# A transformer block on one core: when the transfers are issued, and from which queue

## The chip, the cores and the metric

The kernel runs on one core of one Trainium2 chip. The metric is the time of one execution in device microseconds (us). A core has a matrix engine (PE, with its weight loads as PEld), a vector engine (DVE), a scalar engine (ACT), a general engine (POOL) and a sync engine (SP) that only issues transfers. Each engine takes its instructions strictly in the order of its program. Transfers can be issued by SP and by ACT; in the profile these issues stand under SPq and ACTq.

## The reference

One pre-norm block: attention with 32 heads of 20 columns over a causal window of 256 rows, then a gated feed-forward part. S = 2048 rows, D = 640, F = 1536, all in f32.

```python
def _A_ref(x, wqkv, wo):
    H = 32; Dh = D // H; W = 256
    q, k, v = ...                                   # x @ wqkv, split by heads
    scores = jnp.einsum("bhqd,bhkd->bhqk", q, k) * (Dh ** -0.5)
    mask = (idx[:, None] - idx[None, :] >= 0) & (idx[:, None] - idx[None, :] < W)
    p = _softmax(jnp.where(mask[None, None], scores, -1e9), axis=-1)
    o = jnp.einsum("bhqk,bhkd->bhqd", p, v)
    return o.transpose(0, 2, 1, 3).reshape(B, S, D) @ wo
def _B_ref(x, w_gate, w_up, w_down):
    return (_gelu(x @ w_gate) * (x @ w_up)) @ w_down
h = x + _A_ref(_layernorm(x), wqkv, wo)
out = h + _B_ref(_layernorm(h), w_gate, w_up, w_down)
```

## The kernel before

The rows are cut into 16 blocks of 128 (numbered 0 to 15) and 8 chunks of two blocks. Every f32 operand of a large product is split into two f16 parts, high and low, and a product is made as three f16 products; the weights are split on the chip (`w0h`, `w0l` for q, `w1` for k, `w2` for v, `w3` for the output projection), each scaled by a power of two (`sw`) that is found from its largest element (`am`).

For a chunk the kernel normalizes the rows (`lstx`, `lmvx`, `lyx` are the steps of it, `x_lane` is its code), transposes them on PE (`tp` and, for blocks 1 and 3, `rb`) and splits them into `xh` (a cast on ACT) and `xl` (a difference on DVE). It multiplies by the q and k weights into `mm`, reads the result out as `qks` (high part by ACT, low part by DVE), and writes it to DRAM (`qk00` is chunk 0's q, `qk01` its k, `qk10` chunk 1's q, and so on) by transfers that ACT issues. Six transfers on SP read the q back into `qT`, six the k into `kT`, in the layout that the heads need (`stack`, L654). Two rows of `kT` come from the constant tile `big`, written once. Then a first pass over the scores finds the row maxima (`ra`, `rb` <- `kT`, `qT`; `junk` and `mxs` on DVE), the maxima are added into `qT` as two more rows (`qT<-mT`, issued by ACT), and a second pass makes the scores, the exponentials (`pt`, ACT, with a mask on POOL), and the product with v (`pv`). At the end of a block stand the output projection, the residual (`ht`, loaded again from x, L908) and a store of the sum to `h_dram` (L934). The feed-forward part works from `h_dram`: its first piece beside the last blocks, the rest after about 625 us.

All instructions are recorded through one helper, so the profile gives them all one line, L184; they are told apart by the names of their tiles. The order of each engine is fixed when the program is built. A planner (`Clock`, `Engine.cost`, `Lane.start`) keeps an estimated time for each engine, notes for every region of a tile when it was last written and read (`box`, `note`, `latest`), and issues from a list of generators the first one whose condition (`need`) is met at the estimated time. A generator that only issues transfers yields `("sync",)` and such a condition. So a change of an estimate or of a condition moves instructions on all engines; the estimates are no times of the chip.

One more thing sets the order of transfers. SP and ACT together have eight completion counters, DMAHW0 to DMAHW7, that are given to their transfers in turn, in the order of the plan. A transfer that takes a counter for the second time first waits, on its own engine, until the transfer that had it last has landed. A transfer of SP can so wait for one of ACT, and the other way round; the planner does not count this wait.

At the start SP loads, in this order, x blocks 0 and 1 (`xt`, `pt`), the five slices of the q weights (into `qT`, used as room), five of the k weights (`gu`), x block 2, five of the v weights (`v`), x block 3, then the two transfers `kT<-big`, and when its slots are free slices of the output weights (`wsl`). Block 4's load (`xt`) is a step of the generator `x_lane` for the later blocks.

Of the kernel before, what the change touches and what calls it, by code (L numbers as in the profile page):

```python
# [18 lines left out]
DRAM = bass.MemoryType.DRAM  # L19

S, D, H, DH, F = 2048, 640, 32, 20, 1536
P = 128
# [8 lines left out]
CB = 4  # L31
# [19 lines left out]
class Clock:  # L51
# [16 lines left out]
    @staticmethod  # L68
    def box(ap):

        t = ap.tensor
        size = mybir.dt.size(ap.dtype)
        (ps, pn), *free = [tuple(x) for x in ap.ap]
        if ps:
            p0, f0 = divmod(ap.offset, ps)
        else:
            p0, f0 = 0, ap.offset
        n = 1 + sum((c - 1) * abs(st) for st, c in free)
        step, count = max(((abs(st), c) for st, c in free if c > 1), default=(n, 1))
        run = n - (count - 1) * step  # L80
        if run >= step:
            run, count = n, 1
        return t.name, (p0, p0 + pn, f0 * size, (f0 + n) * size, run * size, step * size, count)
# [91 lines left out]
class Engine:  # L175
# [20 lines left out]
    def cost(self, op, out, ins):  # L196
        n = out.free_size()
        if op == "dma_start":
            size = n * out.partition_size() * mybir.dt.size(out.dtype)
            return size / (300e3 if mybir.dt.size(out.dtype) == 4 else 150e3)  # L200
        half = mybir.dt.size(out.dtype) == 2 and ins and mybir.dt.size(ins[0].dtype) == 2
        if self.name == "tensor":
            n = ins[1].free_size()
            if op == "transpose":
                n = ins[0].partition_size()
            passes = 1 if mybir.dt.size(ins[0].dtype) == 2 else 2 if op == "transpose" else 4
            rows, cols = ins[0].partition_size(), out.partition_size()
            mode = "full" if op == "transpose" else "row" if rows <= 64 else "col"
            mode = "full" if mode == "col" and cols > 32 else mode
            k = self.clock  # L210
            switch, k.mode = SWITCH * (k.mode != mode), mode
            at = (ins[0] if mode == "row" else out).start_partition()
            beside, k.half = mode != "full" and at > k.half and not switch, at
            if beside:
                return 0.004
            return switch + k.warmth(max(n * passes / 2400, 0.027), rows) + 0.0027
        if self.name == "vector":
            m = max([n] + [i.free_size() for i in ins])
            if op == "tensor_copy" and half or op == "tensor_scalar" and m > 320:
                return (0.065 if half else 0.185) + 0.00053 * m  # L220
            return 0.065 + 0.00106 * m + 0.06 * (op == "scalar_tensor_tensor" and len(ins) == 3)
        if self.name == "scalar":
            return 0.00084 * n + (0.05 if op == "copy" or len(ins) == 1 else
                                  0.14 if ins[0].space == PSUM else 0.18)
        if self.name == "gpsimd":
            if op == "memset":
                return 0.06 + 0.0008 * n
            return 0.46 if n == 1 else 0.06 + (0.00105 if op == "affine_select" else 0.00203) * n
        raise NotImplementedError(self.name)
# [3 lines left out]
def block_kernel(ctx: ExitStack, tc: tile.TileContext, x, wqkv, wo, wg, wu, wd, out):  # L233
    nc = Clock(tc.nc)
# [5 lines left out]
    stage = ctx.enter_context(tc.tile_pool(name="stage", bufs=1))  # L240
# [5 lines left out]
    opened, pos = Counter(), Counter()  # L246
# [13 lines left out]
    INF = float("inf")  # L260
# [5 lines left out]
    NR = 4  # L266
    NW, AHEADQ = 3, 6
    SPREAD = 0
    SLICES = 3
# [7 lines left out]
    def need(*reads, slots=(), when=None, eng="tensor"):  # L277

        def f():
            if when and not when() or any(opened[n] >= banks[n] for n in slots):  # L280
                return INF
            return max([nc.ready(reads, eng)]
                       + [nc.slot(psum, n, banks[n]) for n in slots])
        return f
# [4 lines left out]
    def on(eng, *reads, when=None, after=None):  # L289
        f = need(*reads, when=when, eng=eng)  # L290
        if after is not None:
            return (eng,), lambda: max(f(), nc.others(after, eng))
        return (eng,), f
# [18 lines left out]
    class Weight:  # L312
# [21 lines left out]
        def load_slices(self, turn):  # L334
            self.sliced = True
            for i in range(self.shape[0]):
                yield ("sync",), need(when=lambda: pos["taken"] < pos["used"] + SLICES, eng="sync")
                t = nc.tile(stage, [P, D], F32, "wsl", SLICES)[:, :self.shape[1]]
                nc.sync.dma_start(t, self.src[:, i, :])
                self.raw[turn, i] = t  # L340
                pos["taken"] += 1
            self.loaded = True
# [64 lines left out]
    W = {}  # L407
# [125 lines left out]
    RV, RK = 5, 6  # L533
# [50 lines left out]
    def x_lane(blocks, lane):  # L584

        for j in blocks:
            c = C[j // 2]
            if j > 1:
                yield on("vector", when=lambda: W["k"].scaled)
            if j >= NR and j == blocks[0]:  # L590
                yield ("sync",), need(eng="sync", when=lambda: W["v"].scaled)
                load_x(j)
            if j >= NR and j + 1 < NB:
                yield ("sync",), lambda: max(0.0, nc.slot(att, "xt", 2))
                load_x(j + 1)

            def dst():
                if c.x is None:
                    c.x = tuple(nc.tile(wq, [P, KC, CW], F16, n, 3) for n in ("xh", "xl"))
                return tuple(t[:, :, B[j].cols] for t in c.x)  # L600

            yield from layernorm(B[j].x, lane, None, None, dst,
                                 lambda: j < 6 or c.x or C[j // 2 - 3].used == 4,
                                 lambda: B[j].x, tp="rb" if j in (1, 3) else "tp")
            B[j].ready = True

    def load_x(j):
        if 0 < j < NR:
            t = at("pt", [P, 4, 3, P], F32, 3).rearrange("p a b c -> p (a b c)")
            B[j].x = t[:, 0:D]  # L610
        else:
            B[j].x = at("xt", [P, D], F32)
        nc.sync.dma_start(B[j].x, x[j * P:(j + 1) * P, :])
# [38 lines left out]
            side.append((LATE, stack(c, which, d)))  # L652

    def stack(c, which, d):  # L654
        yield ("sync",), need(when=lambda: c < 2 or B[2 * c - 3].scored, eng="sync")
        if which == 0:
            C[c].qT = at("qT", [P, H // 2, CW], F16)
            for b in (2 * c, 2 * c + 1):
                B[b].mx = at("mxs", [P, H], F32, 4)
            to = C[c].qT  # L660
        else:
            s = 2 * c % RK
            to = kT[:, :, s:s + 2, :].rearrange("p i r n -> p i (r n)")
        for par in range(2):
            for m, i in enumerate(((0, 0, 1), (0, 1, 0))[which]):
                rows = slice(64 * par + DH * m, 64 * par + DH * m + DH)
                nc.sync.dma_start(to[rows], d[i].rearrange("(a d i) n -> a d i n", a=2,
                                                           d=DH)[par])
        C[c].stacked += 1
        if C[c].stacked == 2:  # L670
            for b in (2 * c, 2 * c + 1):
                for pr in range(H // 2):
                    heapq.heappush(maxq, (b, pr))
# [89 lines left out]
    row = []  # L763
# [142 lines left out]
        woq.append(j)  # L906

    def residual(j):  # L908
        yield ("sync",), need(when=lambda: j < 2 or B[j - 2].wrote
                              and (j >= CB + 2 or B[j - 2].normed), eng="sync")  # L910
        B[j].h = at("ht", [P, D], F32)
        nc.sync.dma_start(B[j].h, x[j * P:(j + 1) * P, :])

# [11 lines left out]
    def wo_out(j, nh, ps):  # L925
        b = B[j]
        cs = slice(nh * 320, nh * 320 + 320)
        yield on("vector", ps)
        nc.vector.scalar_tensor_tensor(b.h[:, cs], ps, hsc, b.h[:, cs], op0=ALU.mult, op1=ALU.add)
        done("mm")  # L930
        b.halves += 1
        if b.halves < 2:
            return
        nc.sync.dma_start(h_dram[j * P:(j + 1) * P, :], b.h)  # L934
        pos["h"] += 1
        b.wrote = True
# [250 lines left out]
    class Lane:  # L1187
# [11 lines left out]
        def start(self, now):  # L1199
# [11 lines left out]
            if ffpools[1]:  # L1211
                back = FFBACK.get(name, OUT)
            return (all(nc.t[e] <= now + back for e in self.engs if e != "sync")
                    and self.need() <= now + 0.1)

    load_x(0)
    load_x(1)
    qraw = [at("qT", [P, H // 2, CW], F16).bitcast(F32).rearrange("p a n -> p (a n)")
# [2 lines left out]
    for i, n in enumerate("qkv"):  # L1221
        W[n].load(rooms[n])
        if i:
            load_x(i + 1)
    for par in range(2):
        nc.sync.dma_start(kT[64 * par + 60:64 * par + 62].rearrange("p i r n -> p (i r) n"),
                          big[0:2, None, :].to_broadcast([2, RK * H // 2, P]))
    lanes = [x_lane([0], "x"), x_lane([1], "xb"), x_lane([2], "xc"), x_lane([3], "xd"),
             x_lane(range(NR, NB), "x"),
             *(scale_lane([i], str(i)) for i in range(NW)), split_lane(),  # L1230
# [91 lines left out]
```

## Time and profile before

| | |
|---|---|
| three executions, us | 1089.8, 1084.14, 1089.83 (median 1089.8) |
| the profiled execution | 1087.55 us, span of the profile 1085.8 us, mean granted PE clock 0.984 |
| PE busy | 1032.3 us, 95% of the span |
| DVE, ACT, POOL busy | 670.0, 457.1, 173.0 us |
| the chain that ended last | PE 75%, DVE 12%, DMA 6%, ACT 4% of the span |
| transfers | 77.01 MB, 71 GB/s over the span |

The profile is that of one execution. A row of its timeline gives the start, the duration, the engine, the line, the operation and the tiles (out <- in), and in brackets how long the engine had been idle and what it had waited for. A row of SPq or ACTq is an engine that issues transfers (a following `x6` means six of them in a group, and the duration is from the first issue to the end of the last). The clock is the share of full speed that PE was granted.

### The profile page before, as it was taken

How to read it: one execution, taken by the hardware profiler on the slowest of the kernel's cores; microseconds unless marked ns; L12 is line 12 of the kernel's file. 1: busy time of each engine (PE TensorE's matmuls, PEld its weight loads, DVE VectorE, ACT ScalarE, POOL GpSimd, SP SyncE). 2: the span in 40 equal slices, each digit the busy share in tenths (PEclk: the TensorE clock that was granted, in tenths of full speed). 3: DMA queues.
4: the chain of work that ended last, by engine and by line, in shares of the span. 5: the costliest groups of instructions: out<-in, count | busy, mean ns of one | idle time of the engine just before them, and what ended most of it. 6: DMA issues, size and time to landing. Idle time of an engine off the chain costs nothing.

```text
span 1085.8 us, 25031 instructions
## 1 busy us (share of the span) xinstructions
PE 1032.3 (95%) x10122; PEld 631.6 (58%) x10122; DVE 670.0 (62%) x1993; ACT 457.1 (42%) x904; POOL 173.0 (16%) x286
## 2 busy tenths in 40 slices
PE   5368999999999999999999999999999999999998
PEld 3335567666676666676655564555555555545546
DVE  8567899978887687777779389723622263222323
ACT  3213566666666666665767644310211121110110
POOL 1000112332332333333333300000000000000000
PEclk9779999999999999999999999999999999999999
DMA  6526535424233221414052034002000020001001
GB/s 242 137 54 177 130 117 155 128 62 100 64 91 84 73 66 51 88 56 110 34 172 75 14 109 145 1 1 97 1 1 1 25 73 1 1 1 50 1 1 49
DMA packets 63639, 77.01 MB, mean 71 GB/s; under 512 B 6500, under 2 KB 42596, under 8 KB 62564
## 3 DMA queue, kind: packets, MB, share of 16 engines
q1 hardware_dynamic: 40420, 64.67, 20.4%
q10 hardware_dynamic: 23104, 10.75, 3.6%
q8 instruction: 79, 1.29, 0.5%
q14 instruction: 36, 0.29, 0.1%
HBM read 54.07 MB, written 20.97 MB: 69 GB/s over the span
## 4 chain that ended last, share of the span: by engine, by line
PE 75%; DVE 12%; DMA 6%; ACT 4%; issue 2%; SPq 1%; ACTq 0%; POOL 0%; DVEq 0%; POOLq 0%
PE mm L184 57%; PE pv L184 6%; DVE junk L184 4%; PE rb L184 4%; PE tp L184 4%; PE ra L184 4%; ACT pt L184 2%; DMA qk<-qks 2%; DMA kT<-qk 2%; DVE am L184 1%; DMA wsl<-in_wo_dram 1%; DVE qks L184 1%; DVE m L184 1%; SPq L184 1%; DMA qT<-mT 1%
## 5 line engine op out<-in xcount | busy, mean ns | idle before, releaser
L184 POOL TENSOR_SCALAR_AFFINE_SELECT pt<-pt 128x512 f32<-128x512 f32 x240 | 151.3, 653 | 366.8 <-ACT pt L184 365.8
L184 ACT ACTIVATE pt<-rb,esc 128x384 f32<-128x384 f32 (+2 forms) x260 | 132.4, 562 | 75.1 <-PE rb L184 65.1
L184 DVE CUSTOM_DVE_ANT_0 junk<-ra,mask 128x384 bf16<-128x384 f32 (+2 forms) x260 | 137.6, 529 | 42.6 <-PE ra L184 23.2
L184 DVE CUSTOM_DVE_ANT_0 junk<-rb,mask 128x384 bf16<-128x384 f32 (+2 forms) x252 | 133.3, 529 | 48.9 <-PE rb L184 28.7
L184 ACT ACTIVATE pt<-ra,esc 128x384 f32<-128x384 f32 (+2 forms) x252 | 127.5, 559 | 75.0 <-PE ra L184 63.1
L184 DVE SCALAR_TENSOR_TENSOR gel<-mm,ffk,gel 128x512 f32<-128x512 f32 x48 | 35.9, 749 | 145.2 <-PE mm L184 145.1
L184 ACT ACTIVATE gel<-mm,ffk 128x512 f32<-128x512 f32 x48 | 33.0, 687 | 179.1 <-PE mm L184 179.0
L184 PE MATMUL pv<-pt,v 128*21 128x128 f32 x2880 | 104.8, 276 | 0.9 <-ACT oT L184 0.7
L184 DVE SCALAR_TENSOR_TENSOR ht<-mm,ffk,ht 128x320 f32<-128x320 f32 x96 | 52.7, 549 | 79.6 <-PE mm L184 79.4
L184 PEld LDWEIGHTS <-ah 128*128 128x128 f16 x768 | 75.1, 98 | 31.2 <-issue 0.6
L184 ACT CAST ah<-gel 128x512 f16<-128x512 f32 x48 | 29.8, 620 | 128.5 <-DVE gel L184 128.5
L184 PEld LDWEIGHTS pv<-pt,v 128*21 128x21 f32 x2880 | 68.5, 100 | 16.8 <-issue 2.1
L184 PEld LDWEIGHTS <-gu 128*128 128x128 f16 x480 | 45.8, 98 | 51.9 <-issue 0.8
L184 PE MATMUL mm<-hTh,gu 128*128 128x512 f16 x240 | 71.9, 379 | 0.0
L184 PEld LDWEIGHTS <-kT 62*128 62x128 f16 x1440 | 58.9, 95 | 22.1 <-issue 9.6
L184 PEld LDWEIGHTS <-qT 60*128 60x128 f16 x640 | 26.0, 93 | 73.6 <-issue 72.9
L184 PE MATMUL mm<-w2h,xh 128*128 128x320 f16 x160 | 49.4, 309 | 16.8 <-DVE qks L184 16.8
L184 PE MATMUL mm<-xh,w0h 128*128 128x256 f16 x200 | 56.0, 280 | 1.8 <-ACT w0h L184 1.8
L184 PE MATMUL mm<-xh,w0l 128*128 128x256 f16 x200 | 55.9, 280 | 1.0 <-DVE w0l L184 1.0
L184 PE MATMUL mm<-xh,w1h 128*128 128x256 f16 x200 | 54.7, 273 | 1.9 <-DVE qks L184 1.9
L184 PE MATMUL mm<-xl,w0h 128*128 128x256 f16 x200 | 56.0, 280 | 0.0
L184 PE MATMUL mm<-xh,w1l 128*128 128x256 f16 x200 | 54.7, 273 | 0.2 <-DVE w1l L184 0.2
(214 smaller groups left out, 2311.1 us busy)
## 6 DMA issues: line engine op xcount, KB each, us to landing
qk<-qks ACTq DMA_DIRECT2D x64, 128.0 KB
qT<-qk SPq DMA_DIRECT2D x48, 160.0 KB
kT<-qk SPq DMA_DIRECT2D x48, 160.0 KB
ht<-in_x_dram SPq DMA_DIRECT2D x16, 320.0 KB
h_dram<-ht SPq DMA_DIRECT2D x16, 320.0 KB
ht<-h_dram SPq DMA_DIRECT2D x16, 320.0 KB
out_dram<-ht SPq DMA_DIRECT2D x15, 320.0 KB
xt<-in_x_dram SPq DMA_DIRECT2D x13, 320.0 KB
```

Source lines behind the costliest of these rows:

```text
L184: r = real(*args, **kw)
```

## The change

```diff
@@ Clock.box
+        if ap.space == DRAM:
+            n = 1 + sum((c - 1) * abs(st) for st, c in [(ps, pn), *free])
+            return t.name, (0, 1, ap.offset * size, (ap.offset + n) * size, n * size, 1, 1)
@@ Engine.cost
+            rows *= 1 + (mode == "row")
             return switch + k.warmth(max(n * passes / 2400, 0.027), rows) + 0.0027
@@ Weight.load_slices
-                yield ("sync",), need(when=lambda: pos["taken"] < pos["used"] + SLICES, eng="sync")
+                yield ("sync",), lambda: (INF if pos["taken"] >= pos["used"] + SLICES else
+                                          nc.slot(stage, "wsl", SLICES))
@@ x_lane
             if j > 1:
-                yield on("vector", when=lambda: W["k"].scaled)
-            if j >= NR and j == blocks[0]:
-                yield ("sync",), need(eng="sync", when=lambda: W["v"].scaled)
-                load_x(j)
+                yield on("vector", when=lambda: W["k" if j < NR else "v"].scaled)
@@ stack
-        yield ("sync",), need(when=lambda: c < 2 or B[2 * c - 3].scored, eng="sync")
+        yield ("sync",), need(d, when=lambda: c < 2 or B[2 * c - 3].scored, eng="sync")
@@ residual
-        yield ("sync",), need(when=lambda: j < 2 or B[j - 2].wrote
-                              and (j >= CB + 2 or B[j - 2].normed), eng="sync")
+        yield ("sync",), lambda: (INF if j > 1 and not (B[j - 2].wrote and (
+            j >= CB + 2 or B[j - 2].normed)) else nc.slot(att, "ht", 2))
@@ wo_out
+        yield ("sync",), need(b.h, eng="sync")
         nc.sync.dma_start(h_dram[j * P:(j + 1) * P, :], b.h)
@@ block_kernel, start
+    for par in range(2):
+        nc.scalar.dma_start(kT[64 * par + 60:64 * par + 62].rearrange("p i r n -> p (i r) n"),
+                          big[0:2, None, :].to_broadcast([2, RK * H // 2, P]))
     load_x(0)
...
         if i:
             load_x(i + 1)
-    for par in range(2):
-        nc.sync.dma_start(kT[64 * par + 60:64 * par + 62].rearrange("p i r n -> p (i r) n"),
-                          big[0:2, None, :].to_broadcast([2, RK * H // 2, P]))
+    load_x(NR)
```

Four things are edited. (1) The planner's region of a DRAM tile is now its true range of bytes, and a matmul in row mode (64 rows or fewer) counts double towards the estimated warmth of PE. (2) Slices of weights (`wsl`), the reads of q and k (`stack`), the residual's load (`ht`) and the store to `h_dram` are issued by the plan only once their source, or the slot that they go into, is estimated ready; before, they stood in SP's order as soon as the program's own condition held. (3) Block 4's load (`load_x(NR)`) is issued right behind the weights' loads at the start. (4) The two transfers `kT<-big` are issued by ACT, as the first two in the program, and no longer by SP behind the loads.

Since the planner's estimates change, the order of instructions changes on all engines. ACT at the start, before, with what each row waits for (PE_49, Pool_49 and so on are the counters of the engines):

```order
L184 ACT_TABLE_LOAD
L184 CAST xh<-tp 128x4x128 [waits PE_49]
L184 CAST xh<-tp 128x128 [waits PE_49]
L184 CAST xh<-rb 128x4x128 [waits PE_49]
L184 CAST xh<-rb 128x128 [waits PE_49]
```

and now:

```order
L187 DMA kT<-big 2x96x128 [waits DMAHW0_49,Pool_49]
L187 DMA kT<-big 2x96x128 [waits DMAHW0_49]
L187 ACT_TABLE_LOAD
L187 CAST xh<-tp 128x4x128 [waits PE_49]
L187 CAST xh<-tp 128x128 [waits PE_49]
```

The two transfers stand ahead of the table load and the first cast of `xh`. By the counters' turns the second one has the third turn of DMAHW0, behind x block 0, the first `kT<-big` and the third slice of the v weights; it waits until that slice has landed.

SP where it reads chunk 4's k back, before (the names end in numbers of instances; `kT_108` is the one `kT`):

```order
L184 DMA kT_108<-qk41_3769 20x16x256 [waits DMAHW7_49]
L184 DMA kT_108<-qk41_3769 20x16x256 [waits DMAHW1_49]
L184 DMA kT_108<-qk41_3769 20x16x256 [waits DMAHW2_49]
L184 DMA kT_108<-qk41_3769 20x16x256 [waits DMAHW3_49]
L184 DMA kT_108<-qk41_3769 20x16x256 [waits DMAHW4_49]
L184 DMA kT_108<-qk41_3769 20x16x256 [waits DMAHW5_49]
```

and now:

```order
L187 DMA kT_108<-qk41_3701 20x16x256 [waits DMAHW0_49]
L187 DMA kT_108<-qk41_3701 20x16x256 [waits DMAHW2_49]
L187 DMA kT_108<-qk41_3701 20x16x256 [waits DMAHW3_49]
L187 DMA kT_108<-qk41_3701 20x16x256 [waits DMAHW6_49]
L187 DMA kT_108<-qk41_3701 20x16x256 [waits DMAHW7_49]
L187 DMA kT_108<-qk41_3701 20x16x256 [waits DMAHW0_49]
```

Before, the fourth and fifth of these wait, through DMAHW3 and DMAHW4, for ACT's writes of a group of chunk 5's q (`qk50`). Now the fifth waits, through DMAHW7, for a write of a group of chunk 5's k (`qk51`), and the sixth follows it.

PE just before the first row of maxima of block 8 (the first product of chunk 4's `kT` and `qT`), before, from the last products with v on:

```order
L184 MATMUL pv_111<-pt_5353,v4_107 21x128 x4
L184 MATMUL pv_111<-pt_5353,v1_104 21x128 x4
L184 LDWEIGHTS ol_5197
L184 MATMUL mm_5432<-w3h_1151,ol_5197 128x320
L184 LDWEIGHTS oh_5196
L184 MATMUL mm_5432<-w3h_1151,oh_5196 128x320
L184 LDWEIGHTS oh_5196
L184 MATMUL mm_5432<-w3l_1152,oh_5196 128x320
L184 LDWEIGHTS ol_5197
L184 MATMUL mm_5432<-w3h_1151,ol_5197 128x320
L184 LDWEIGHTS qT_5090
L184 MATMUL rb_5526<-kT_108,qT_5090 128x384
```

and now:

```order
L187 MATMUL pv_111<-pt_5368,v0_103 21x128 x4
L187 MATMUL pv_111<-pt_5368,v4_107 21x128 x4
L187 MATMUL pv_111<-pt_5368,v1_104 21x128 x4
L187 MATMUL tp_5536<-ident_73,xt_4040 128x128 x4
L187 LDWEIGHTS w1h_306
L187 MATMUL mm_5542<-xh_3705,w1h_306 128x256
L187 LDWEIGHTS qT_5120
L187 MATMUL rb_5547<-kT_108,qT_5120 128x384
```

The output projection's products (`mm<-w3`, `oh`) no longer stand there. Between the last matmul that the late `kT` reads wait for (by way of a write of ACT) and the first row of maxima of the chunk, PE now has 81, 87, 94 and 106 matmuls in chunks 2, 3, 4 and 5; before it had 170, 285, 136 and 134. What the reads wait for there now is ACT's `qT<-mT` in chunk 2 and writes of the next chunk's k or q in chunks 3, 4 and 5. In the same way PE now has 219 matmuls ahead of the first row of maxima of block 0, before 174.

## The prediction

> **What bounds the kernel now.** I read the table of busy time by stretch first (columns: length, then busy time of PE, PEld, DVE, ACT, POOL with counts, the granted PE clock, the DMA share and GB/s).
>
> ```profile
> 0.00:25.00 25.00, 11.93 (x63) 7.28 (x64) 20.77 (x55) 7.43 (x12) 3.04 (x11) 1.00 0.72 257
> 25.00:50.00 25.00, 11.83 (x106) 10.11 (x104) 12.31 (x30) 8.64 (x14) 1.06 (x2) 0.84 0.58 150
> 50.00:75.00 25.00, 13.56 (x75) 7.46 (x75) 15.68 (x64) 4.21 (x9) 1.78 (x6) 0.61 0.27 58
> 75.00:100.00 25.00, 21.98 (x180) 14.32 (x178) 18.53 (x82) 4.80 (x12) 1.19 (x2) 1.00 0.50 140
> 125.00:350.00 225.00, 221.47 (x3036) 152.86 (x3035) 194.51 (x653) 145.60 (x307) 65.68 (x106) 1.00 0.37 101
> 350.00:550.00 200.00, 198.09 (x2922) 131.51 (x2920) 147.99 (x501) 132.00 (x269) 62.98 (x103) 1.00 0.26 66
> 625.00:1085.00 460.00, 457.34 (x2587) 254.20 (x2584) 189.02 (x393) 89.04 (x146) 7.40 (x12) 1.00 0.09 33
> ```
>
> Two regimes. In the first 100 us PE is idle 41 of them; DVE, with 21 of the first 25 us, and the transfers set the pace. From 125 us on PE is busy 98 to 99% of each stretch, so there a stall of PE is lost whole, and nothing but PE's own work can be won. The matmuls are the same before and after, so the change can win only in the ramp and lose anywhere.
>
> The timeline of the ramp, by engine (ACT, DVE, PE, then SP), holds the waits that the change touches.
>
> ```profile
> 0.80 1.28 ACT L184 ACT_TABLE_LOAD   x1 [0.80 <-PEq L1309]
> 9.11 0.59 ACT L184 CAST xh<-tp 128x512 f16<-128x512 f32 x1 [7.03 <-PE tp L184]
> 23.56 1.10 ACTq L184 DMA_DIRECT2D qk<-qks  x2
> 40.07 13.52 ACTq L184 DMA_DIRECT2D qk<-qks  x2
> 53.63 0.83 ACT L184 ACTIVATE w2h<-v,sw 128x640 f16<-128x640 f32 x1 [12.88 <-DVE qks L184]
> 10.40 0.68 DVE L184 TENSOR_TENSOR xl<-tp,xh 128x512 f16<-128x512 f32 x1
> 36.83 0.15 DVE L184 TENSOR_SCALAR sw<-pw 128x1 int32<-128x1 int32 x1
> 49.61 0.49 DVE L184 BATCH_NORM_STATS2 lstx<-xt 128x6 f32<-128x320 f32 x1 [12.62 <-DMA xt<-in_x_dram]
> 53.24 0.42 PE L184 MATMUL mm<-w2h,xh 128*128 128x320 f16 x1 [14.23 <-DVE qks L184]
> 60.68 0.26 PE L184 MATMUL rb<-kT,qT 60*128 60x128 f16 x1 [4.35 <-DMA kT<-qk]
> 64.59 0.26 PE L184 MATMUL rb<-kT,qT 60*128 60x128 f16 x1 [3.65 <-DMA kT<-qk]
> 14.49 11.58 SPq L184 DMA_DIRECT2D kT<-big  x2
> 25.42 0.65 SPq L184 DMA_DIRECT2D kT<-big  x1
> 44.24 0.83 SPq L184 DMA_DIRECT2D xt<-in_x_dram  x2
> ```
>
> DVE stands still for 12.62 us from 36.98 to 49.61, for block 4's x, which SP issues only at 44.24. PE's 14.23 us before 53.24 are the shadow of that. Then come 4.35 and 3.65 us for chunk 0's k.
>
> **Block 4's load.** It now goes out with the weights' loads and is there long before DVE wants it: the wait of 12.62 us goes, and the order of DVE's first 90 rows is otherwise the same. Term: -12.6. As the price of one more load in front, at about 400 GB/s (row below) 320 KB take 0.8 us, behind everything that DVE needs early: 0.
>
> **kT<-big on ACT.** The second of these transfers has the third turn of a counter and waits until the third v slice has landed. The trace shows both halves of what follows. First, SP's second `kT<-big` stood from about 15 to 25.42 for a counter, until ACT's first write, issued at 23.56, had landed, and SP issued nothing else meanwhile. Second, ACT does the same: a write issue that began at 40.07 with the next in its group held ACT until 53.6, and `w2h`, which came next, had 12.88 us of idle time before it, though its own input had landed long before. So ACT will issue nothing from the start until that slice lands. When is that?
>
> ```profile
> GB/s 0 0 154 287 396 307 256 229 324 399 362 399 406 413 406 410 406 393 393 399 399 396 382 406 289 127 40 0 0 0 0 0 94 195 62 29 19 19 63 131
> 13.60 0.33 SPq L184 DMA_DIRECT2D pt<-in_x_dram  x1
> ```
>
> (The first row is the DMA rate over 0 to 30 us in 40 slices.) Each of these issues by SP waits for the load eight places ahead: the issue at 13.60 shows the 11th load landed, the one at 14.49 the 12th. The third v slice is the 16th, at 0.82 us each (320 KB at 400 GB/s): 14.49 + 4 x 0.82 = 17.8. From there, the issue itself 0.65 (as SP's at 25.42), the table load 1.28, which was hidden at 0.80 and now is not, and the first cast 0.59: `xl` on DVE can start at about 20.3 in place of 10.40. DVE's rows up to there are done and the next wait in order behind it; up to 36.98 DVE has hardly a gap. Term: +9.9. Bounds: +8.5 if the slice comes a microsecond sooner and DVE's half-microsecond gaps are used up, +12 if the small descriptors of `kT<-big` hold the loads up. Together the two edits leave -2.7 at the point where DVE goes on with block 4.
>
> **Chunk 0's k and the rest of the ramp.** PE now has 45 more matmuls ahead of block 0's first maxima. They can run in the 8.0 us in which it waited for `kT`, whose reads move by the same -2.7. But DVE's order and work remain, and DVE, busy 16 to 19 of 25 us there, must serve the same readouts. Bounds 0 and -8.0; I take -1.6, near the DVE end, since after 75 us the gaps of PE are short and DVE's work sets the blocks' rhythm. A later gap, at 96.5, is for output weights that SP had issued late:
>
> ```profile
> 96.50:99.50 3.00, 0.82 (x8) 0.59 (x6) 1.09 (x2) 0.59 (x2) 0.00 (x0) 1.00 1.00 335
> 99.50:104.00 4.50, 4.12 (x26) 2.06 (x25) 3.48 (x16) 1.01 (x3) 0.64 (x1) 0.62 0.77 231
> ```
>
> The slices move about behind chunk 1's reads; 2.2 us may go or come: 0, with -2.2 and +2.2 as bounds. The ramp thus gives -4.3.
>
> **The reads of chunks 2 to 5.** This term decides. `stack` now waits for the estimated landing of the writes, so the reads stand later in SP's order, beside writes of ACT whose counters they share, and the planner does not see that wait. Before, chunk 4 shows what such a wait costs.
>
> ```profile
> 319.02 0.60 ACT L184 ACTIVATE qks<-mm 128x512 f16<-128x512 f32 x1 [0.17 <-PE mm L184]
> 319.73 4.72 DMA qk<-qks
> 326.04 6.03 DMA kT<-qk
> 317.70 9.08 SPq L184 DMA_DIRECT2D kT<-qk  x6
> 318.90:332.85 13.95, 13.50 (x198) 1.00 0.61 124
> 89.85 0.26 ACT L184 COPY mT<-tp 64x128 f16<-64x128 f16 x1 [2.94 <-DMA qk<-qks]
> 90.14 1.90 ACTq L184 DMA_DIRECT2D qT<-mT  x2
> 90.14 3.23 DMA qT<-mT
> ```
>
> (ACT's readout, two steps of the chain, SP's issues, the busy time of the stretch, and three rows of the ramp on `mT`.) PE ends the group at 318.9; ACT reads it out, its write takes 4.72, the last read is issued at 326.04 and lands at 332.07: 13.1 us from PE's last matmul. The 136 to 140 matmuls that PE had in between lasted 13.5 us, so the chain was just covered (0.45 us idle): 0.097 us a matmul. In the changed kernel PE has 81, 87, 94 and 106 there, which is 7.9, 8.4, 9.1 and 10.3 us. Against them stand, in chunk 2, a chain through `qT<-mT`: copy 0.3, the second of two issues 1.3 after the first, landing 3.23 and the read 6.03, together 10.9, less some overlap of the issues, 10.4: stall 2.5. Before, three of chunk 4's reads came behind the wait, 0.8 us apart; now one does in chunk 3, 13.1 - 1.6 = 11.5 against 8.4, and two in chunks 4 and 5, 12.3 against 9.1 and 10.3: stalls of 3.1, 3.2 and 2.0. Sum +10.8. Bounds: if all four ran the full 13.1, 52.4 - 35.7 = +16.7; if a matmul's share there were a third longer (+11.9 of cover), 0. The 0.45 us of before go: -0.4.
>
> **The clock.** Behind the gap of 2.2 us at 96.5 the granted clock was 0.62 over the next 4.5 us, in which PE was busy 4.12: 4.12 x 0.38 = 1.6 us lost. By that row three of the four stalls are long enough, 4.8 us; one gap can't tell how often it happens, and I count two: +3.2 (bounds 0 and 6.4). The Trainium skill, "TensorE: Matmul & The Clock Gate", section "Why this matters for your kernels", warns of PE gaps over about 3 us between bursts, since the clock then falls back to half; the trace shows 0.62 after a gap shorter than that. By the page's figure the last rival below, which counts all four, would count three of its gaps (chunk 5's is 2.8 there) and end 1.6 us lower.
>
> Twenty-one more changes of tile mode on PE, nearly all in the ramp, are at 0 beside the waits there (bound +2, at the 0.097 of a matmul each). The other edits (`ht`, `h_dram`, late `wsl`) move transfers that nobody waits for: SP's own waits are not the kernel's, and from 625 us PE has 2.7 us idle of 460.
>
> **Sum:** -4.3 - 0.4 + 10.8 + 3.2 = +9.3. The profiled execution took 1087.55, of which 1.75 lie outside the span of 1085.8; it stands 2 under the median of 1089.8 and on the mean of the three executions, 1087.9. So 1087.55 + 9.3 = 1097. About 0.5%, 5.4 us, is what a measurement of this kernel can tell from no change: against 1087.9 that is 1082.5 and 1093.3.
>
> **The rivals.**
> Faster, because the reads of chunks 2 to 5 are covered: PE's work between gate and first maximum is longer than 0.097 a matmul (the stretches hold more 320-column products), or the late counters are free sooner. It decides if the four stalls stay under about 1 us each. Then there is no clock loss, and if half of the 8.0 us for chunk 0's k goes too: 1087.55 - 2.7 - 4 - 0.4 = 1080.5. For it: chunk 4 was covered by chance already. Against: its lead falls by a third. Chance 0.24.
> The two sides cancel: stalls of half the size and one loss of clock, 1087.55 - 4.3 - 0.4 + 5.4 + 1.6 = 1089.9. Chance 0.22.
> ACT is not held: the second `kT<-big` goes out early and its wait harms nobody, so that 9.9 us less are spent: 1087 with my stalls, 1071 without. Against it is the row at 53.63. The same page of the Trainium skill ("TensorE: Matmul & The Clock Gate", section "Architectural detail") calls ACT's queue a strict FIFO, which the row bears out. Chance 0.07.
> Slower still: each of the four stalls cools the clock and the chains run the full 13.1: -4.3 - 0.4 + 16.7 + 6.4 = +18.4, 1106. Chance 0.11.
> My forecast, 1097 (1092 to 1102): 0.36.
>
> Slower by over 0.5%: the last rival 0.11, seven tenths of the forecast 0.26 and some of the cancelling case 0.04, 0.41. Faster: 0.22 of the first rival and 0.05 of the one on ACT, 0.27. The rest, 0.32, is within. The range from 1078 to 1105 leaves out the lowest of the third rival and half of the fourth.
>
> **What the profile of the changed kernel would show.** The first cast of `xh` on ACT near 19.7, behind two ACTq rows, and DVE idle for some 9 us before `xl`; no wait of DVE for x in 35 to 60; block 0's first maxima near 62. Rows of PE `<-DMA kT<-qk` of 2 to 4 us before the first maxima of blocks 4, 6, 8 and 10, and a clock under 1.00 behind the longest. It would be wrong if the cast stays near 9, or if those rows are missing between 125 and 400 us.

## The result and the profile after

The changed kernel takes 1114.1 us (median of 6, 1110.95 to 1116.94) against 1089.5 before (median of 6): ratio 1.0238, 95% interval 1.0210 to 1.0266. It is slower, by 25 us where 9 were forecast, and lies outside the range of 1078 to 1105.

PE's busy time in three stretches of the two profiled executions (columns: length, PE busy, clock, DMA share, GB/s), first before, then after:

```profile
0.00:125.00 125.00, 81.99 (x612) 0.86 0.54 152
125.00:650.00 525.00, 517.93 (x7088) 1.00 0.32 87
650.00:1085.80 435.80, 432.35 (x2426) 1.00 0.08 28
```

```profile
0.00:125.00 125.00, 82.59 (x541) 0.88 0.52 146
125.00:650.00 525.00, 502.92 (x6986) 0.99 0.32 82
650.00:1111.00 461.00, 457.56 (x2599) 1.00 0.10 34
```

In the ramp PE idles as long as before, 42.4 us against 43.0, but it has 71 fewer matmuls done at its end. Between 125 and 650 us it idles 22.1 us against 7.1. Behind that it has the same 3.4 us of idle time; the work only comes 25 us later. So the loss is made before 650 us.

The two profiles hold the same 10122 matmuls, and their spans differ by 25.3 us. Of that, 14.5 us are idle time of PE and 10.8 us are longer busy time, which is mostly the clock. As an estimate, take PE's busy time times the share of the clock that it was not granted, summed over stretches of 5 us: 7.0 us before, all in the ramp, and 15.9 us after, 12.4 in the ramp and 3.5 in the middle. One stretch of the ramp shows it, before and then after (columns as in the prediction's table):

```profile
70.00:85.00 15.00, 14.66 (x114) 8.40 (x113) 11.74 (x68) 2.23 (x5) 0.55 (x1) 1.00 0.18 47
```

```profile
70.00:85.00 15.00, 14.97 (x72) 5.69 (x71) 11.73 (x72) 1.18 (x2) 0.55 (x1) 0.50 0.11 34
```

PE is busy all the time in both and DVE does as much; at half clock PE gets through 72 matmuls in place of 114.

The timeline of the ramp after, ACT, DVE, PE, SP, then two steps of the chain:

```profile
3.93 17.77 ACTq L187 DMA_DIRECT2D kT<-big  x2
21.73 1.28 ACT L187 ACT_TABLE_LOAD   x1 [21.73 <-DMA v<-in_wqkv_dram]
23.02 0.58 ACT L187 CAST xh<-tp 128x512 f16<-128x512 f32 x1
23.64 0.69 DVE L187 TENSOR_TENSOR xl<-tp,xh 128x512 f16<-128x512 f32 x1 [12.97 <-ACT xh L187]
50.15 0.48 DVE L187 BATCH_NORM_STATS2 lstx<-xt 128x6 f32<-128x320 f32 x1
64.10 0.21 PE L187 MATMUL ra<-kT,qT 60*128 60x128 f16 x1 [2.00 <-DMA kT<-qk]
67.86 0.28 PE L187 MATMUL ra<-kT,qT 60*128 60x128 f16 x1 [3.55 <-DMA kT<-qk]
18.03 1.28 SPq L187 DMA_DIRECT2D v<-in_wqkv_dram  x3
3.93 14.08 DMA kT<-big
18.03 3.02 DMA v<-in_wqkv_dram
```

ACT stands from 3.93 to 21.7, as forecast in kind, but 3.3 us longer: the first `kT<-big`, 48 KB, itself takes 14.08 us beside the loads, and the third v slice waits for its counter until 18.03. `xl` comes at 23.64 (10.40 before). DVE's wait for block 4's x is gone, and its first row there stands at 50.15, where before it stood at 49.61: the two edits cancel.

The waits of PE in the middle, and the two stretches of 25 us in which the granted clock fell:

```profile
211.01 0.48 PE L187 MATMUL ra<-kT,qT 60*128 60x384 f16 x1 [5.07 <-DMA kT<-qk]
287.08 0.21 PE L187 MATMUL ra<-kT,qT 60*128 60x128 f16 x1 [2.42 <-DMA kT<-qk]
643.80 0.85 PE L187 MATMUL pv<-pt,v 128*21 128x128 f32 x24 [2.64 <-ACT oT L187]
200.00:225.00 25.00, 18.53 (x247) 11.65 (x245) 13.19 (x45) 13.27 (x28) 6.13 (x11) 0.86 0.55 108
275.00:300.00 25.00, 22.25 (x287) 14.24 (x288) 18.90 (x65) 12.30 (x28) 6.64 (x12) 0.93 0.48 107
```

Chunks 2 and 3 wait, chunks 4 and 5 don't. The chain and SP's row show why chunk 2's wait is twice the forecast:

```profile
193.46 5.10 DMA qk<-qks
198.58 4.72 SPq L187 DMA_DIRECT2D kT<-qk  x6
202.56 8.32 DMA kT<-qk
```

All six reads are issued behind the write, and the last takes 8.32 us (6.03 for the last one of chunk 4 before). SP issues weight slices right behind it, from 203.40 on; that they slow it is likely, not shown.

### The profile page after: what moved, and what is told of

Same layout as the page of the kernel before. It is cut to its first block, busy times and chain, and to the rows that moved or that the text cites. A ratio compares the mean times of both kernels' runs of the same rounds, so it can differ in the third digit from the quotient of the medians.

```text
span 1111.1 us, 25020 instructions
## 1 busy us (share of the span) xinstructions
PE 1043.1 (94%) x10122; PEld 633.6 (57%) x10122; DVE 675.9 (61%) x1993; ACT 457.0 (41%) x904; POOL 171.2 (15%) x286
## 4 chain that ended last, share of the span: by engine, by line
PE 78%; DVE 9%; DMA 6%; ACT 3%; issue 2%; SPq 1%; ACTq 0%; POOL 0%; DVEq 0%; POOLq 0%
PE mm L187 59%; PE pv L187 6%; PE tp L187 4%; PE rb L187 4%; PE ra L187 4%; DVE junk L187 3%; DMA kT<-qk 3%; ACT pt L187 1%; DMA qk<-qks 1%; DMA kT<-big 1%; DVE m L187 1%; DVE am L187 1%; SPq L187 1%; DMA qT<-mT 1%; DVE o L187 1%
## 5 line engine op out<-in xcount | busy, mean ns | idle before, releaser
L187 DVE CUSTOM_DVE_ANT_0 junk<-rb,mask 128x384 bf16<-128x384 f32 (+2 forms) x266 | 141.2, 531 | 46.1 <-PE rb L187 24.1
L187 ACT ACTIVATE pt<-ra,esc 128x384 f32<-128x384 f32 (+2 forms) x264 | 135.0, 565 | 81.6 <-PE ra L187 68.1
L187 ACT ACTIVATE pt<-rb,esc 128x384 f32<-128x384 f32 (+2 forms) x248 | 124.8, 556 | 89.2 <-PE rb L187 71.6
L187 DVE CUSTOM_DVE_ANT_0 junk<-ra,mask 128x384 bf16<-128x384 f32 (+2 forms) x246 | 130.1, 529 | 51.5 <-PE ra L187 27.4
L187 PE MATMUL ra<-kT,qT 60*128 60x384 f16 (+2 forms) x308 | 43.5, 296 | 16.3 <-DMA kT<-qk 14.9
```

Of the source, the lines that this page charges most:

```text
L187: r = real(*args, **kw)
```

## The experiments

The runs are called e1 to e17. Times are medians in us; each ratio is to the kernel before, run on the same chip at the same time (its medians 1086.5 to 1087.0), with its 95% interval. "PE's order unchanged" holds for all its instructions.

**ACT's issue.** Two kernels take it out of the changed kernel (e1, e2), one puts it alone into the kernel before (e3).

```diff
-        nc.scalar.dma_start(kT[64 * par + 60:64 * par + 62]...     # first in the program
+        nc.sync.dma_start(kT[64 * par + 60:64 * par + 62]...       # e1: SP, behind load_x(NR)
+        nc.gpsimd.dma_start(kT[64 * par + 60:64 * par + 62]...     # e2: POOL, first
```

> The changed kernel with the two kT<-big transfers back on SP, behind the loads; every other instruction of every engine stands where it stood in the changed kernel. Theory (ACT held until the third v slice lands shifts the whole ramp): the first cast on ACT comes near 9 in place of 23.0, DVE's 13 us of idle time before xl go, and the time falls by 10 to 14 us from 1114, to 1100-1104. Rival (the ramp has slack elsewhere, and the loss is in the later order alone): at most 3 us less, 1111 or more.

> The changed kernel with the two kT<-big transfers issued by POOL, whose transfers use other counters; nothing else moved. Theory: ACT is free as in the run with SP, 1100-1104. If the transfers' many small pieces slow the loads beside them, it is 1 to 3 us slower than the run with SP. Rival (what matters is that the transfer runs beside the loads, not who issues it): 1110 or more.

> The kernel before with one edit: the two kT<-big transfers are ACT's first instructions; the rest of the order is that of before. Theory: the first cast comes at 20 to 23 and everything behind it, block 4's late load too, moves by 11 to 13 us: 1100-1103. Rival (DVE's 12.6 us of waiting for block 4 take the shift up, since SP is not held): 1090.

On SP (e1): 1105.3, ratio 1.0169 (1.0152 to 1.0187). On POOL (e2): 1103.1, 1.0152 (1.0114 to 1.0190). So ACT's hold costs 0.7% here, some 7.5 us, a little under the expected 10; when POOL issues the small pieces beside the loads, the time shows no cost of it. Into the kernel before (e3): 1088.4, 1.0013 (0.9999 to 1.0027), the rival:

```profile
18.01 1.28 ACT L184 ACT_TABLE_LOAD   x1 [18.01 <-DMA kT<-big]
19.92 0.69 DVE L184 TENSOR_TENSOR xl<-tp,xh 128x512 f16<-128x512 f32 x1 [9.46 <-ACT xh L184]
57.04 0.43 PE L184 MATMUL mm<-w2h,xh 128*128 128x320 f16 x1 [7.90 <-DVE qks L184]
```

The shift of 9.5 us at `xl` is there, and PE's wait for the work behind block 4's load shrinks from 14.23 to 7.90 us. So the hold costs time in the changed kernel, where block 4's x is already there, and none that can be seen in the kernel before, where DVE waits for that x anyway.

**Block 4's load alone, and with the waits of the plan.**

```diff
-            if j >= NR and j == blocks[0]:
-                yield ("sync",), need(eng="sync", when=lambda: W["v"].scaled)
-                load_x(j)
...
+    load_x(NR)                                       # e4; e5: also need(d), ht, h_dram
```

> The kernel before with one edit: block 4's load goes out with the weights' loads; PE's order is unchanged. Theory: DVE's wait of 12.6 us goes and the time falls by 9 to 13 us, to 1077-1081. Rival (DVE's wait covered the wait for chunk 0's k, which stays where it is): 4 us less or none, 1085-1089.

> The kernel before with block 4's load early and three of the new waits of the plan (reads of q and k, residual's load, store to h_dram), without the exact DRAM regions and without the new condition for the weight slices. PE's order is that of the kernel before. Theory (the loss comes from PE's new order, which only the regions and the slices' condition bring about): as the kernel with block 4's load alone, 1079 to 1082. Rival (the later reads themselves cost, through the shared counters): 1085 or more.

e4: 1080.5, 0.9943 (0.9926 to 0.9960). e5: 1081.4, 0.9957 (0.9940 to 0.9974). Half of the 12.6 us comes through, because PE then waits for chunk 0's k, 12.64 us where it was 4.35 (e4):

```profile
55.45 0.26 PE L184 MATMUL rb<-kT,qT 60*128 60x128 f16 x1 [12.64 <-DMA kT<-qk]
```

The new waits of `stack`, `residual` and `wo_out` change nothing that can be seen by themselves.

**That wait.** Two attempts to shorten it, with PE's order unchanged: `kT<-big` on POOL (e8), and chunk 0's six `kT` reads on POOL (e12).

> The kernel before with block 4's load early and the two kT<-big transfers issued by POOL; the order of PE, DVE and ACT is unchanged. Theory (in the kernel with block 4's load alone, PE waits 12.6 us for chunk 0's k, whose reads stand on SP behind the second kT<-big and the weight slices): SP reaches the reads sooner, 2 to 5 us less than 1080.5, 1075 to 1079. Rival (the reads wait for their own writes by ACT): 1080 to 1082.

> The kernel before with block 4's load early (1080.5), and chunk 0's six kT reads issued by POOL and no longer by SP, where they stand behind the q reads. The order of PE, DVE and ACT is unchanged. Theory (the 12.6 us that PE waits at 43 to 55 us are SP's queue): the wait shrinks by 3 to 6 us and the time to 1075-1078. Rival (POOL issues slower than SP, or the reads wait for the last write anyway): 1080 to 1083.

e8: 1079.8, 0.9928 (0.9905 to 0.9950), no better than e4 that can be told. The time is the rival's, but the wait does shrink as the theory has it, from 12.64 to 8.46 us; the work ahead of it comes later (the first product with `w2h` at 44.07, in e4 at 40.60), so block 0's first maxima start only 0.7 us sooner. e12: 1083.3, 0.9967 (0.9953 to 0.9982), 2.8 us over e4 with intervals that just overlap; the wait grows to 14.74 us, so here the rival holds. e4 and e8 are the fastest kernels of this study.

**The regions.** Added to e4 (e6); taken out of the changed kernel (e9). A lead, here and below, is the number of matmuls that PE has between the last one that a chunk's late `kT` reads wait for and the chunk's first row of maxima.

```diff
+        if ap.space == DRAM:
+            n = 1 + sum((c - 1) * abs(st) for st, c in [(ps, pn), *free])
+            return t.name, (0, 1, ap.offset * size, (ap.offset + n) * size, n * size, 1, 1)
```

> The kernel before with block 4's load early and the exact DRAM regions. PE's order changes: 222 matmuls ahead of block 0's first maxima (174 before, 219 in the changed kernel), but the reads of k for chunks 2 to 5 keep leads of 120 matmuls and more. Theory (PE runs 17 us at half clock behind block 0's first maxima, since the dense products that would go with them have been used up): the half clock from 60 to 77 us is there, no wait for kT in chunks 2 to 5, 1086 to 1092. Rival (my prediction's: the reads of chunks 2 to 5 are nearly the whole loss): 1079 to 1083.

> The changed kernel without the exact DRAM regions; all its other edits stay, kT<-big on ACT too. PE's order becomes that of the kernel with block 4's load and the slices' condition (1093). Theory (the regions bring the short leads): no wait for kT in chunks 2 to 5, and with ACT held by up to 9 us 1093 to 1102. Rival (the regions do nothing by themselves in the whole change, the new conditions do): 1110 to 1116.

e6: 1139.6, 1.0490 (1.0457 to 1.0522), 59 us over e4, far beyond both expectations. The leads that the expectation names belong to a neighbouring kernel; in this one the last reads of chunks 2 to 7 have 62, 76, 40, 192, 31 and 60 matmuls, and PE waits in each of these chunks, here in chunks 4 and 6 (the first row names a load of x, which SP issued 0.8 us behind the last `kT` read):

```profile
350.75 0.47 PE L187 MATMUL rb<-kT,qT 60*128 60x384 f16 x1 [6.60 <-DMA xt<-in_x_dram]
492.99 0.26 PE L187 MATMUL rb<-kT,qT 60*128 60x128 f16 x1 [5.28 <-DMA kT<-qk]
```

e9: 1102.0, 1.0139 (1.0121 to 1.0156): 1.0% off the changed kernel, and no PE wait for `kT` over 0.7 us between 125 and 500 us; a wait of 5.04 us for DVE's `mxs` at 200.26 stays, which e7 below explains. PE's order is then e7's, matmul for matmul. The regions bring the short leads.

They bring the half clock of the ramp too. By the estimate of the section on the result, the nine kernels with the regions lose 10.2 to 13.1 us to the clock in their first 125 us, and the ten without them (e9 among these, with 4.1) lose 3.2 to 7.0.

**The late reads.** The changed kernel with `kT<-big` on SP, without the condition that my prediction blamed.

```diff
-        yield ("sync",), need(d, when=lambda: c < 2 or B[2 * c - 3].scored, eng="sync")
+        yield ("sync",), need(when=lambda: c < 2 or B[2 * c - 3].scored, eng="sync")
```

> The changed kernel with kT<-big on SP (1105) and without the new condition on the reads of q and k, which my prediction blamed. The matmuls between the last wait of the kT reads and the chunk's first maxima are then 23, 23, 22 and 65 in chunks 1 to 4 (37, 81, 87 and 94 with the condition). Theory (what counts is that lead, and the condition makes it longer): waits of 4 to 7 us for kT in each of chunks 1 to 4, each with 3 to 7 us of half clock behind it, 1120 to 1135. Rival (my prediction's step: the condition makes the reads late): 1092 to 1100.

1115.0, 1.0255 (1.0228 to 1.0281), slower than e1 by 9.7 us. Its longest waits for `kT` are 6.9, 5.3, 5.8 and 4.2 us in chunks 1 to 4. The size is under the expected 1120, the sign is the theory's: beside the regions, the condition helps.

**The weight slices.** Their condition alone, added to e4 (e7); taken out of e1 (e15); and with the condition, the slices issued by POOL, in e7's kernel (e16) and in e1's (e17).

```diff
-                yield ("sync",), need(when=lambda: pos["taken"] < pos["used"] + SLICES, eng="sync")
+                yield ("sync",), lambda: (INF if ... else nc.slot(stage, "wsl", SLICES))   # e7
-                nc.sync.dma_start(t, self.src[:, i, :])
+                nc.gpsimd.dma_start(t, self.src[:, i, :])                                  # e16, e17
```

> The kernel before with block 4's load early and the new condition for the weight slices alone. The ramp of PE up to block 1 is that of before; later the order differs, with leads of 103 to 130 matmuls for the last reads of chunks 1, 3, 4 and 7. Theory (a lead of over 100 matmuls is nearly enough): 1079 to 1085. Rival (each such read stalls PE by 2 us or more and cools its clock): 1088 or more.

> The kernel with block 4's load early and the slices' condition (1093), with the weight slices issued by POOL, whose transfers use other counters than SP's and ACT's; the order of PE, DVE and ACT is unchanged. Theory (the planner counts a slice as issued in time, but on SP it stands behind a counter that a write of ACT holds, and DVE then waits 6.6 us for it near 189): that wait of DVE and PE's 7.2 us near 193 are gone, 1080 to 1086. Rival (the slice is late by the plan itself): the wait stays, 1090 to 1095.

> The changed kernel with kT<-big on SP (1105), with the weight slices issued by POOL; the order of PE, DVE and ACT is unchanged. Theory (the kT reads of chunks 2 and 3 wait for counters held by slices and writes, and share the transfer engines with the slices): PE's waits near 200 and 277, 4.7 and 3.0 us, shrink to half or less, 1093 to 1101. Rival (the reads wait for their own late writes): they stay, 1103 to 1107.

> The changed kernel with kT<-big on SP (1105) and without the new condition for the weight slices. The last kT reads have leads of 32, 120, 135, 196, 108 and 81 matmuls in chunks 1 to 6. Theory (leads of 100 and more are covered, a slice that comes late holds DVE in order): waits for kT only in chunks 1 and 6, no wait of DVE for wsl near 190, 1088 to 1096. Rival (the regions alone carry the loss): 1103 to 1107.

e7: 1093.0, 1.0062 (1.0036 to 1.0088), 12.5 us over e4. The rival's time, but by another way than it said, a slice that DVE waits for (chain, DVE, PE):

```profile
181.91 7.35 DMA qk<-qks
189.88 0.69 DVE L184 TENSOR_REDUCE am<-wsl 128x1 f32<-128x512 f32 x1 [6.62 <-DMA wsl<-in_wu_dram]
193.23 0.26 PE L184 MATMUL rb<-qT,kT 62*128 62x128 f16 x1 [7.15 <-DVE mxs L184]
```

SP stands behind ACT's write until 189.3, the slice lands late, and DVE, in order, holds the maxima with `am`. With the slices on POOL (e16): 1086.8, 0.9997 (0.9981 to 1.0013), and both waits are gone; 6 us of the 12.5 went with the slices' place on SP and its counters. In e1's kernel (e17): 1097.9, 1.0118 (1.0087 to 1.0150), 7.3 us less by the medians and 5.5 by the ratios; the wait near 200 is gone, of 3.0 us near 277 2.47 stay. e15: 1098.0, 1.0105 (1.0083 to 1.0127), a little over its range; PE still waits 4.76 us in chunk 1 and 5.55 in chunk 2, the latter in spite of a lead of 120 matmuls. The profile names a slice of `wu` as what ended it, but the product needs the last `kT` read: SP had issued it by 198.2, and PE starts 9.6 us later, with slices issued from 198.3 on. So lead alone doesn't tell the wait.

**The clock.** Twenty extra products in e1's kernel, before the wait for `kT` (e11) and behind block 0's first maxima (e13); and one long wait put into e4 by repeating chunk 4's last read (e14).

```diff
+                for _ in range(warm if i == 0 and k == 0 else 0):
+                    nc.tensor.real.matmul(o, l, r, start=True, stop=True)      # e11, e13: warm = 20
+        for _ in range(8 if (c, which) == (4, 1) else 0):
+            nc.sync.real.dma_start(to[rows], src)                              # e14
```

> The changed kernel with kT<-big on SP (1105), and 20 more products of 256 columns, whose result is overwritten, in front of the first group of chunk 1's q, just behind block 0's first maxima; nothing else moves. They are extra work of 4.3 us at half clock. Theory (the clock stays at half from 60 to 77 us because PE changes between short maxima and two or three products, and a straight run releases it): full clock from about 64, and in spite of the extra work 2 to 5 us less, 1100 to 1103. Rival (DVE sets the pace there, the half clock costs nothing): 0 to 4 us more, 1105 to 1109.

> The changed kernel with kT<-big on SP (1105), with the 20 extra products of 256 columns now behind block 0's first two pairs of maxima (in front of the second half of the first group of chunk 1's q); in the run before they stood in front of the wait for kT. Extra work of 4.3 us at half clock, their result is overwritten. Theory (alternating maxima and products keep the half clock, a straight run releases it): full clock from 66 in place of 76, and 1 to 4 us less than 1105 in spite of the extra work. Rival (the half clock from 60 to 76 costs nothing, or a straight run doesn't release it): the half clock stays to 76 or later, 1105 to 1110.

> The kernel before with block 4's load early (1080.5), and the last of chunk 4's kT reads issued nine times in a row (the same bytes to the same place): all eight counters go round once, and the data counts as landed some 7 us later. It prices one wait of PE in the middle of the kernel. Theory (a wait costs itself and then half of some 7 us at half clock): a wait W of 6 to 9 us for kT near 328 us, granted clock 0.5 for 4 to 7 us behind it, and the time longer by W + 3, 1089 to 1093. Rival (the wait alone): W longer, 1086 to 1090, clock 1.00 behind it.

e11: 1104.7, 1.0165 (1.0146 to 1.0183), and it tells nothing, since the products ran in the idle time ahead of the wait. e13: 1107.5, 1.0186 (1.0168 to 1.0204), 2 us over e1, with intervals that overlap:

```profile
61.91 3.85 PE L495 MATMUL mm<-xh,w0h 128*128 128x256 f16 x20
66.00:69.00 3.00, 2.77 (x22) 1.00 0.00 0
69.00:72.00 3.00, 2.43 (x15) 0.97 0.15 44
72.00:75.00 3.00, 3.00 (x15) 0.50 0.16 46
78.00:81.00 3.00, 3.00 (x16) 0.50 0.38 109
```

Behind the straight run the clock is full from 66, but by 72 it has fallen back, and while it is full PE idles 0.8 us of 6. The time is the rival's. What a full clock would be worth there isn't shown: the 3.85 us of extra work cost about 2, so the 6 us of full clock gave back some 2, which the noise could hide.

e14: the repeats waited for one another, so the wait became 30 us and not 7; 1114.0, 1.0247 (1.0230 to 1.0265):

```profile
355.59 0.50 PE L184 MATMUL rb<-kT,qT 60*128 60x384 f16 x1 [30.44 <-DMA kT<-qk]
355.00:360.00 5.00, 4.41 (x32) 0.61 0.45 147
360.00:365.00 5.00, 5.00 (x92) 1.00 0.10 27
```

The time grows by 33.5 us over e4 for a wait of 30.44. The 3 us above it are the theory's size, but the intervals are as wide; the clock of 0.61 over 4.41 us accounts for 1.7.

## Why the prediction was wrong

By edits, from ratio to ratio: block 4's load -0.6% (e4), with the slices' condition +1.2 (e7), with the regions and the rest +1.1 (e1), with ACT's issue +0.7: 1.0238. These shares depend on the order of the edits: the regions alone cost 5.5% on e4 (e6), and e1 without the slices' condition gains 0.6% (e15).

By place, the sum had -4.3 us for the ramp and +13.6 for the middle (10.8 + 3.2 - 0.4). The two profiles give about +5 for the ramp (0.6 us less idle time, 5.4 more lost to the clock), +18.5 for the middle (15.0 idle, 3.5 clock) and 2 that are not placed. Two steps failed most: the ramp, whose half clock the sum doesn't have, and the late weight slices, put at nothing.

1. **Block 4's load, -12.6:** mis-sized. Alone it gives 6.3 us; the wait for chunk 0's k takes the other half (e4).
2. **kT<-big on ACT, +9.9:** right in mechanism, too small at its place: 13.2 us at `xl`, above the bound of 12. The first `kT<-big` took 14.08 us and held the counter of the third v slice. The turns of DMAHW0 told ahead of the prediction have it there (the second `kT<-big` is the fourth on that counter, behind three landings); the prediction timed the slice by the rate of the loads alone. "Together -2.7" measured +0.5. At the end the hold costs 7.5 us, and nothing that can be seen in the kernel before (e3).
3. **The ramp, -4.3: this step failed.** Block 0's first maxima came near 64, not 62, and at 125 us nothing was won. The wait of 14.23 us behind block 4's x went, but one of 15.06 for `xl`, before 24.39, took its place. Then PE ran at half clock from 68 to 86 us, where before it had 1.00 from 70 to 100. In these kernels that comes with the regions' order of PE's instructions; why that order keeps the clock low stays open. Without the hold a gain is there in spite of it: in e1 PE is busy 90.9 of the first 125 us, against 82.
4. **The reads of chunks 2 to 5, +10.8:** 7.5 us of waits (5.07 and 2.42, none in chunks 4 and 5). That the size nearly fits is partly luck: one wait is twice its forecast and two stayed away, and why leads of 94 and 106 were enough stays open. The cause that I named fell: the new condition in `stack` is harmless (e5) or helps (e10); the exact regions bring the order (e6, e9). I read the order rightly and put the blame on the wrong line. The other half of the 15.0 us of idle time in the middle are waits that the sum doesn't have; the longest is 2.64 us for `oT` before 643.80.
5. **"Late `wsl` move transfers that nobody waits for": this step failed.** A term put at nothing costs 12.5 us alone (e7), and 5.5 to 7.3 in the changed kernel (e15, e17). DVE waits for the slices, in order, and PE for DVE (e7); and when POOL issues them, a wait for `kT` goes as well (e17). Whether SP's queue, the shared counters or the shared transfer engines made that one isn't separated.
6. **The clock, +3.2:** 18.53 x 0.14 + 22.25 x 0.07 = 4.2 us in the two stretches shown, 3.5 by the finer estimate. The size is right for the middle; the 5.4 us of the ramp are not in it. The Trainium skill, "TensorE: Matmul & The Clock Gate", section "Why this matters for your kernels", gives about 3 us of idle time as the limit; here the gap of 2.42 us alone lies in the stretch with 0.93.

What stays open: e17, with SP's `kT<-big` and POOL's slices, is still 17 us over e4. Between their two profiles, 15.0 us apart, PE idles 6.2 us less in the ramp and 12.4 more between 125 and 650 us, and its busy time is 8.3 us longer, 5.7 of it clock. Which edit makes these waits was not measured apart. The doubled count of row-mode matmuls was never run alone; e6 and e15 differ by it and the three waits of e5, and lie 42 us apart, of which e10 gives some 10 to the reads' condition. That the regions' effect comes from a truer estimate of landing was not tried.

## What to carry to other kernels

A transfer that is issued "just in time" has no reserve for waits that the plan doesn't know, as the weight slices here; where two engines share completion counters in turn, a transfer can wait for one that it has nothing to do with, so count that wait or leave the issue early. A transfer put in front of a compute engine's program can hold the whole engine: ask which transfer had its counter before, and when that one lands. When one wait is removed, look for the next thing that the same work needs, as chunk 0's k here, before counting the gain. When an order changes, compare the granted clock too, and not idle time alone: PE's busy time grew by 10.8 us here with the same matmuls.

## What the runs showed of the hardware

A transfer of 48 KB in 192 pieces of 256 bytes took 14.08 us beside loads of 320 KB that landed 0.8 to 1.0 us apart. PE's clock can stay at half while PE is busy nearly without a gap: in the changed kernel it is 0.50 from 70 to 85 us, with PE busy 14.97 of the 15 us in pairs of 60-row maxima and mostly two to four products between them. In e13 a run of 20 products in a row was followed by 1.00 from 66 us on; by 72 it was 0.50 again, after 0.8 us of idle time in 6.
